# Attention, a Fourier mix and a feed-forward on one core: queries and keys loaded into both halves of the partitions, and weights that start later

## The chip, the core and the metric

The kernel runs on one core of a Trainium2 chip. Its engines work side by side, each through its own instruction stream in order: TensorE (PE, with its weight loads listed apart as PEld), VectorE (DVE), ScalarE (ACT), GpSimd (POOL) and SyncE (SP). SP, ACT and POOL also issue DMA transfers; 16 DMA engines carry them. The metric is the time of one execution on the device in microseconds (us); lower is better.

## The reference

For 8 batches of 8 heads, q, k and v are 576 x 64 in float32. Each head is attention with a mask by blocks of 64 rows; the heads side by side give x, 576 x 512 a batch. Then comes a two-dimensional Fourier transform of which the real part is added to x, a normalization and a feed-forward of 512 to 2048 to 512:

```python
scores = np.where(block_i >= block_j, q @ k.T / 8, -1e9)     # blocks of 64
attn = softmax(scores) @ v
x = attn.transpose(0, 2, 1, 3).reshape(B, S, H * D)
u = x + np.real(np.fft.fft(np.fft.fft(x, axis=1), axis=2))
un = (u - mean(u)) / np.sqrt(var(u) + 1e-6)
out = u + np.maximum(un @ w_ch1, 0) @ w_ch2
```

## The kernel before

**Precision.** TensorE gets rounded operands, so nearly every operand is held as a rounded part and the rest: probabilities, values, normalized rows and both weights as pairs of float16 (hi and lo), q and k as pairs of fp32r. A product is three matmuls (hi hi, hi lo, lo hi); for scores two suffice, since the pairs lie one above the other in the 128 partitions.

**A head.** `load_head` (L311) loads q and k of a head, transposed, 64 partitions x 1152 (288 KB). `lead` (L316) rounds both on ACT into LEAD, partitions 0 to 63; partitions 64 to 67 hold the mask. `lead_copies` (L319) copies the rounded q and k by two DMAs on SP into REST, each to the half in which the other's remainder will stand. `rest` (L324) writes the remainders there: q's on DVE, k's on POOL. LEAD and REST have two buffers, by the head's parity. `scores` (L391) multiplies REST with REST and LEAD with LEAD into PSUM, takes maxima on DVE (L411 to L416), exponentials on ACT twice (L425: float16 and float32) and their difference on POOL (L426). `turn` (L428) transposes the pair of float16 by a DMA on SP. `values` (L435) multiplies by the values' pair and scales by the sums of the rows (L463 to L466). After the second head of a pair the two columns go to x in DRAM (L471, L474).

**A batch.** When a batch's last pair is stored, `mirror` (L517) loads x again, plainly and with rows mirrored by indirect DMAs on POOL. `folded`, `stage1`, `stage2_sin` and `stage2_cos` (L538 to L632) do the transform over half the frequencies; the last step adds sums and differences to x: four additions a group, three groups a batch (L623 to L626), on DVE for batch 0 and on POOL for the others. `normalized_steps` (L670) normalizes and transposes on PE; each pair of row tiles then becomes a feed of 16 steps (`feed_steps`, L717), whose matmuls (h and acc) fill PE.

**The weights.** They are loaded as 64-bit words in 18 pieces (`weight_loads`, L813, from ACT), at most three ahead, into parts of W that are not yet needed and, for the last four, into `stage`. `weight_single` (L822) makes float32 of a piece in three DVE operations (L828 to L830) and sums its squares on ACT (L831). `weight_scale` (L836) gets a scale from the sums (once a weight), and `weight_parts` (L851) splits each of 2 x 16 chunks into hi and lo: the first weight by ACT, ACT and POOL (L855 to L859), the second by ACT and DVE (L855, L861). The first feed needs these chunks; heads of the second batch are not written before the last piece is (`"w32"`, L922).

**The order.** All this is written by a planner (L261 to L304, L910 to L958): lanes of steps with assumed costs for each engine and latencies ("D0.6" is 0.6 us of DVE, "L2.5" a latency of 2.5 us), keys that a step makes, keys that it comes after, and a place by which lanes are ranked. A step is issued when its assumed time has come; weights are squeezed in where DVE's or ACT's assumed queue is short. The framework then orders each engine's instructions once more by a simulation of its own, with the written order as rank and the data as the only hard condition. Matmuls alone keep the written order (`mm`, L201).

Of the kernel before, what the change touches and what calls it, by code (L numbers as in the profile page):

```python
# [37 lines left out]

FLIGHT = 3

PSHIFT = 5
# [144 lines left out]
def tile_attn_fourier_ffn(  # L186
# [14 lines left out]
    def mm(*args, **kw):  # L201
        return tc.keep_in_program_order(nc.tensor.matmul(*args, **kw))  # L202
# [28 lines left out]
    NB = 2  # L231
    LEAD = [const.tile([KM, 64 + 2 * S], F32R, name=f"lead{i}") for i in range(NB)]
    REST = [const.tile([P, 64 + 2 * S], F32R, name=f"rest{i}") for i in range(NB)]
    PROB = [[const.tile([P, 2, w], F16, name=f"prob{i}_{x}") for i, w in enumerate(WIDTHS)] for x in range(2)]
# [5 lines left out]
    for i in range(NB):  # L240
        nc.gpsimd.dma_start(LEAD[i][D:KM], c_masks)
        nc.vector.tensor_scalar(LEAD[i][0:D, 0:64], ones[0:D, 0:64], 0.0, None, op0=ALU.mult)
        nc.vector.tensor_scalar(REST[i][:, 0:64], ones[:, 0:64], 0.0, None, op0=ALU.mult)
    for n, blocks in enumerate(BLOCKS):
# [66 lines left out]
    def load_head(h):  # L311

        raws[h] = work.tile([D, 2 * S], F32, name="raw", bufs=2)
        nc.sync.dma_start(raws[h], qk[h])

    def lead(h):  # L316
        nc.scalar.copy(LEAD[h % NB][0:D, 64:], raws[h])  # L317

    def lead_copies(h):  # L319
        x0, x1 = REST[h % NB].bitcast(F32), LEAD[h % NB].bitcast(F32)  # L320
        nc.sync.dma_start(x0[D:P, 64:64 + S], x1[0:D, 64:64 + S])
        nc.sync.dma_start(x0[0:D, 64 + S:], x1[0:D, 64 + S:])

    def rest(h, which):  # L324

        x0, x1, raw = REST[h % NB], LEAD[h % NB].bitcast(F32), raws[h]
        if which == 0:
            nc.vector.tensor_tensor(x0[0:D, 64:64 + S], raw[:, 0:S], x1[0:D, 64:64 + S], op=ALU.subtract)  # L328
        else:
            nc.gpsimd.tensor_tensor(x0[D:P, 64 + S:], raw[:, S:], x1[0:D, 64 + S:], op=ALU.subtract)  # L330

# [59 lines left out]
    def scores(h, n):  # L391

        x0, x1 = REST[h % NB], LEAD[h % NB]
        prob = PROB[h % 2][n]
# [3 lines left out]
        for parts in SCORES[n]:  # L398
            t = ps_tile()
            at = 0  # L400
            for i, (j, lo, hi) in enumerate(parts):
                q, k = slice(P * j, P * (j + 1)), slice(64 + S + lo, 64 + S + hi)
                to = t[:, at:at + hi - lo]
                mm(to, x0[:, q], x0[:, k], start=(i == 0), stop=False, skip_group_check=True)
                mm(to, x1[:, q], x1[:, k], start=False, stop=(i == len(parts) - 1), skip_group_check=True)
                places.append((j, lo, hi, to))
                at += hi - lo
# [27 lines left out]
    def values(h, at):  # L435
# [32 lines left out]
        )  # L468
        if hh == 1:
            ds = slice(D * (n - 1), D * (n + 1))  # L470
            nc.sync.dma_start(  # L471
                xd[64:576, ds].rearrange("(c p) d -> p c d", p=P), x[:, 1:5].rearrange("p c h d -> p c (h d)")
            )
            nc.sync.dma_start(xd[0:64, ds], x[64:128, 0].rearrange("p h d -> p (h d)"))  # L474

# [19 lines left out]
    def value_lane():  # L495
        for h in range(B * H):
            for n in range(3):
                yield Step(
                    lambda n=n: values(h, n), (0.75, 0.38, 0.29)[n], ("D0.95",) if n == 2 else (),
                    (("S", h, n), ("N", h // 2)) + ((("V", h - 1, 2),) if h else ()), ("V", h, n),  # L500
                    need=(("d", h // H - 3, "u"),) if n == 2 and h >= 3 * H else (), place=h + 0.5,
                )
# [11 lines left out]
    def fourier_steps(b):  # L514
# [93 lines left out]
        def stage2_cos(c):  # L608
# [27 lines left out]
        yield Step(  # L636
            mirror, 0.0, ("G3", "L2.5"), (("V", H * b + H - 1, 2),), D_("u"),
            need=(("F", feed_number(b - 2, 1)),) if b > 1 else (), place=place,
# [14 lines left out]
        for c in (2, 0, 1):  # L653
            yield Step(lambda: stage2_sin(c), 0.67, ("A0.38",), (D_("zs"),), D_("b", c), True, place=place)
            yield Step(
                lambda: stage2_cos(c), 0.78, ("D0.86", "B", "D1.66" if b == 0 else "G3.0"), (D_("zc"), D_("zt"), D_("b", c)), D_("u", c), True,
                need=(("F", feed_number(b - 1, 2)),) if c == 2 and b == 4 else (), place=place,
            )
# [154 lines left out]
    def weight_loads(done):  # L813
# [6 lines left out]
        loads[0] = x  # L820

    def weight_single(x):  # L822
        if loads[0] <= x:
# [85 lines left out]

    lanes = [head_lane(), prepare_lane(), v_lane(), score_lane(), turn_lane(), value_lane(), transform_lane()]  # L910
    heads = [next(x) for x in lanes]
# [93 lines left out]
```

## Time and profile before

| what | value |
|---|---|
| median of 3 runs (lowest to highest) | 1315.21 us (1314.83 to 1320.55) |
| profiled execution: time, span | 1318.01 us, 1316.2 us |
| mean granted TensorE clock | 0.966 |
| busy: PE, DVE, ACT, POOL | 1125.2, 713.2, 620.6, 549.0 us |
| moved by DMA | 161.77 MB, of it 135.94 by SP's queue |

How to read it: busy times are sums over the span, and engines overlap. A row of the timeline gives start and length in us, engine, line, operation, output<-input, shape and count; brackets give the engine's idle time before it and what ended that. A name with q (SPq, ACTq) is an engine's sequencer, here mostly issuing DMAs. The DMA share is the mean busy share of the 16 DMA engines. L202 is the helper through which all matmuls are recorded, so they are told apart by tiles: ps, h and acc (PSUM banks, which scores also borrow), av for attention times values, wst for the weights' scale.

### The profile page before, as it was taken

The numbers are of one execution on the slowest core, as the hardware profiler recorded it, in microseconds if no ns is written. First come the engines' busy times: TensorE is split into PE (matmuls) and PEld (weight loads), VectorE is DVE, ScalarE is ACT, GpSimd is POOL, SyncE is SP. The second block draws the span as 40 slices with busy tenths as digits, with TensorE's granted clock in tenths as the row PEclk, the third lists the DMA queues.
The fourth block names the chain that finished last, engine by engine and source line by source line (L and its number), as shares of the span: only waits on it lengthen the run. The fifth ranks groups of instructions, "written<-read, shape, count | busy, mean of one in ns | idle before, by whom it ended". The sixth has DMA issues, their size and how long they took to land.

```text
span 1316.2 us, 25240 instructions
## 1 busy us (share of the span) xinstructions
PE 1125.2 (85%) x9620; PEld 826.4 (63%) x9620; DVE 713.2 (54%) x1697; ACT 620.6 (47%) x1329; POOL 549.0 (42%) x715
## 2 busy tenths in 40 slices
PE   1344175798989898989999999999999999999998
PEld 1244154575767676667767677667667767767665
DVE  7954477646465755576656656674673432412211
ACT  3645747764456543655666545665562211111110
POOL 2635725554455553536655366645741500300000
PEclk9999986798999998999999999999999999999999
DMA  9999607987568745765898567985863000000000
GB/s 320 230 203 237 176 5 141 163 172 151 96 148 152 172 85 130 144 152 116 173 193 165 108 120 191 173 167 114 172 119 82 26 16 17 21 1 17 16 17 16
DMA packets 307178, 161.77 MB, mean 123 GB/s; under 512 B 259281, under 2 KB 277857, under 8 KB 306929
## 3 DMA queue, kind: packets, MB, share of 16 engines
q1 hardware_dynamic: 300416, 135.94, 51.1%
q10 hardware_dynamic: 4384, 16.78, 3.9%
q0 software_dynamic: 2256, 7.45, 1.8%
q8 instruction: 75, 1.23, 0.4%
q14 instruction: 47, 0.38, 0.1%
HBM read 58.37 MB, written 18.87 MB: 59 GB/s over the span
## 4 chain that ended last, share of the span: by engine, by line
PE 52%; DVE 9%; DMA 8%; POOL 3%; issue 3%; ACT 2%; SPq 0%; DVEq 0%; POOLq 0%; ACTq 0%
PE h L202 20%; PE acc L202 20%; PE ps L202 8%; DMA turn<-prob 6%; PE av L202 3%; DVE M L411 2%; DMA u<-xd,rows 1%; DVE rest L328 1%; DVE tmp L541 1%; POOL prob L426 1%; PE ps L205 1%; ACT prob L425 1%; POOL rest L330 1%; ACT p L425 1%; DVE tmp L542 1%
## 5 line engine op out<-in xcount | busy, mean ns | idle before, releaser
L202 PE MATMUL h<-uh,W 128*128 128x256 f16 x2304 | 424.7, 276 | 0.0
L426 POOL TENSOR_TENSOR prob<-p,prob 128x288 f16<-128x288 f32 (+4 forms) x384 | 286.9, 754 | 276.2 <-ACT p L425 259.4
L202 PEld LDWEIGHTS <-W 128*128 128x128 f16 x3456 | 332.9, 99 | 67.1 <-issue 4.7
L202 PE MATMUL acc<-W,gh 128*128 128x512 f16 x1152 | 348.4, 384 | 0.0
L202 PE MATMUL h<-ul,W 128*128 128x256 f16 x1152 | 317.5, 276 | 0.0
L425 ACT ACTIVATE prob<-ps,M 128x64 f16<-128x64 f32 (+2 forms) x358 | 164.6, 493 | 138.6 <-DVE M L416 137.3
L742 DVE SCALAR_TENSOR_TENSOR gl<-h,gh 128x512 f16<-128x512 f32 x144 | 99.0, 687 | 238.6 <-ACT gh L741 238.2
L202 PE MATMUL acc<-W,gl 128*128 128x512 f16 x576 | 220.7, 383 | 1.1 <-DVE gl L742 0.6
L202 PE MATMUL av<-VH,turn 128*128 128x65 f16 x1920 | 130.7, 205 | 96.9 <-DMA turn<-prob 82.2
L741 ACT ACTIVATE gh<-h 128x512 f16<-128x512 f32 x144 | 86.7, 602 | 269.0 <-PE h L202 268.4
L202 PEld LDWEIGHTS <-turn 128*128 128x128 f16 x2880 | 116.9, 105 | 126.0 <-DMA turn<-prob 98.7
L411 DVE TENSOR_REDUCE M<-ps 128x1 f32<-128x288 f32 (+2 forms) x358 | 138.8, 426 | 88.1 <-PE ps L202 72.5
L425 ACT ACTIVATE p<-ps,M 128x64 f32<-128x64 f32 (+2 forms) x358 | 171.1, 494 | 15.1 <-POOL prob L426 12.5
L202 PEld LDWEIGHTS <-gh 128*128 128x128 f16 x1152 | 105.7, 100 | 97.1 <-issue 9.9
L330 POOL TENSOR_TENSOR rest<-raw,lead 64x576 fp32r<-64x576 f32 x64 | 106.9, 1671 | 115.7 <-ACT lead L317 89.4
L202 PE MATMUL ps<-rest 128*128 128x288 f32 (+2 forms) x358 | 123.7, 363 | 34.2 <-ACT p L425 26.6
L202 PE MATMUL av<-VL,turn 128*128 128x64 f16 x960 | 118.6, 204 | 0.0
L202 PEld LDWEIGHTS ps<-rest 128*128 128x128 f32 x358 | 73.8, 206 | 47.2 <-ACT p L425 32.3
L202 PE MATMUL ps<-lead 68*128 68x288 f32 (+2 forms) x358 | 103.3, 322 | 0.0
L202 PEld LDWEIGHTS <-gl 128*128 128x128 f16 x576 | 56.9, 99 | 71.5 <-issue 2.7
L317 ACT CAST lead<-raw 64x1152 fp32r<-64x1152 f32 x64 | 73.5, 1149 | 18.6 <-PE ps L202 18.4
L202 PEld LDWEIGHTS ps<-lead 68*128 68x128 f32 x358 | 74.3, 208 | 1.3
(166 smaller groups left out, 1197.2 us busy)
## 6 DMA issues: line engine op xcount, KB each, us to landing
raw<-in_qk_dram SPq DMA_DIRECT2D x64, 288.0 KB
rest<-lead SPq DMA_DIRECT2D x128, 144.0 KB
W<-in_moe_w_ch_dram ACTq DMA_DIRECT2D x14, 1024.0 KB
V<-in_v_dram SPq DMA_DIRECT2D x32, 320.0 KB
xd<-x SPq DMA_DIRECT2D x32, 256.0 KB
out_dram<-u SPq DMA_DIRECT2D x32, 256.0 KB
u<-xd SPq DMA_DIRECT2D x8, 512.0 KB
turn<-prob SPq DMA_TRANSPOSE x192
```

What stands on the lines that cost most here:

```text
L202: return tc.keep_in_program_order(nc.tensor.matmul(*args, **kw))
L205: return tc.keep_in_program_order(nc.tensor.transpose(*args, **kw))
L317: nc.scalar.copy(LEAD[h % NB][0:D, 64:], raws[h])
L328: nc.vector.tensor_tensor(x0[0:D, 64:64 + S], raw[:, 0:S], x1[0:D, 64:64 + S], op=ALU.subtract)
L330: nc.gpsimd.tensor_tensor(x0[D:P, 64 + S:], raw[:, S:], x1[0:D, 64 + S:], op=ALU.subtract)
L411: nc.vector.tensor_reduce(m[:, i:i + 1], x, axis=AX.X, op=ALU.max)
L425: nc.scalar.activation(to, x, AF.Exp, bias=bias[:, c:c + 1], scale=0.125)
L426: nc.gpsimd.tensor_tensor(pl, p32, ph, op=ALU.subtract)
L541: nc.vector.tensor_tensor(e[0:r], X[c][0:r], U[c][0:r], op=op)
L542: nc.vector.tensor_tensor(e[0:r, 1:256], e[0:r, 1:256], e[0:r, 511:256:-1], op=op)
L741: nc.scalar.activation(gh, t, AF.Relu)
L742: nc.vector.scalar_tensor_tensor(gl, t, 0.0, gh, op0=ALU.max, op1=ALU.subtract)
```

## The change

- The host hands q and k over twice, one below the other, and `load_head` loads 128 partitions (576 KB) instead of 64.
- `lead` rounds all 128 partitions into ONE (the old REST). The two DMA copies go. `lead_q` writes the rounded q into TWO (the old LEAD) by a copy on DVE from the raw q; `rest` writes q's remainder over the second half of ONE (DVE) and k's into TWO (POOL). Scores multiply ONE with ONE and TWO with TWO.
- Storing a pair of heads becomes a step of its own (`store_x`), in a lane of its own; a batch's `mirror` comes after the last of them, and the next pair's last `values` step after the one before.
- `weight_begin` writes one element of each of the first three landing places on DVE, from the raw tile of head 1 or the first V, so that these loads wait for those two. In the planner, piece x (0 to 7) is ranked after the last scores of head x (`AFTER`).
- The additions of batch 0 move from DVE to POOL.

```diff
+AFTER = (0, 1, 2, 3, 4, 5, 6, 7)
...
-        raws[h] = work.tile([D, 2 * S], F32, name="raw", bufs=2)
+        raws[h] = work.tile([P, 2 * S], F32, name="raw", bufs=2)
         nc.sync.dma_start(raws[h], qk[h])
     def lead(h):
-        nc.scalar.copy(LEAD[h % NB][0:D, 64:], raws[h])
-
-    def lead_copies(h):
-        x0, x1 = REST[h % NB].bitcast(F32), LEAD[h % NB].bitcast(F32)
-        nc.sync.dma_start(x0[D:P, 64:64 + S], x1[0:D, 64:64 + S])
-        nc.sync.dma_start(x0[0:D, 64 + S:], x1[0:D, 64 + S:])
+        nc.scalar.copy(ONE[h % NB][:, 64:], raws[h])
+
+    def lead_q(h):
+        nc.vector.tensor_copy(TWO[h % NB][0:D, 64:64 + S], raws[h][0:D, 0:S])
     def rest(h, which):
-        x0, x1, raw = REST[h % NB], LEAD[h % NB].bitcast(F32), raws[h]
+        x, raw = ONE[h % NB].bitcast(F32), raws[h]
         if which == 0:
-            nc.vector.tensor_tensor(x0[0:D, 64:64 + S], raw[:, 0:S], x1[0:D, 64:64 + S], op=ALU.subtract)
+            nc.vector.tensor_tensor(ONE[h % NB][D:P, 64:64 + S], raw[D:P, 0:S], x[D:P, 64:64 + S], op=ALU.subtract)
         else:
-            nc.gpsimd.tensor_tensor(x0[D:P, 64 + S:], raw[:, S:], x1[0:D, 64 + S:], op=ALU.subtract)
+            nc.gpsimd.tensor_tensor(TWO[h % NB][0:D, 64 + S:], raw[0:D, S:], x[0:D, 64 + S:], op=ALU.subtract)
...
-            yield Step(lambda: lead_copies(h), 0.0, ("Q1.2", "L2.2"), (("T", h),), ("TC", h), place=h - 0.9)
+            yield Step(lambda: lead_q(h), 0.0, ("D0.6",), (("L", h),), ("TC", h), place=h - 0.9)
...
+    def store_x(g):
+        b, n = divmod(2 * g, H)
+        xd, x, ds = xs[b], xs["pair"], slice(D * n, D * (n + 2))
+        nc.sync.dma_start(
+            xd[64:576, ds].rearrange("(c p) d -> p c d", p=P), x[:, 1:5].rearrange("p c h d -> p c (h d)")
+        )
+        nc.sync.dma_start(xd[0:64, ds], x[64:128, 0].rearrange("p h d -> p (h d)"))
+
+    def store_lane():
+        for g in range(B * H // 2):
+            yield Step(lambda: store_x(g), 0.0, ("Q1.1", "L2.0"), (("V", 2 * g + 1, 2),), ("XS", g), place=2 * g + 1.6)
...
-            engine = nc.vector if b == 0 else nc.gpsimd
+            engine = nc.gpsimd
...
+    def weight_begin():
+
+        for x in range(FLIGHT):
+            nc.vector.tensor_copy(raw(x)[0:1, 0:1].bitcast(F32), (raws[1][0:1, 0:1], vraw[0][0:1, 0, 0, 0:1])[x % 2])
+        weight_loads(0)
+
...
-        yield Step(lambda: weight_loads(0), 0.0, ("A1.2", "L5"), (("L", 0),), ("load",))
+        yield Step(weight_begin, 0.0, ("D0.4", "A1.2", "L6"), (("L", 1), ("LV", 0)), ("load",))
...
-                (("load",),), "w32" if x == len(LANDS) - 1 else None,
+                (("load",),) + ((("E", AFTER[x], 2),) if x < len(AFTER) else ()), "w32" if x == len(LANDS) - 1 else None,
...
+    qk = np.concatenate([qk, qk], 1)
```

More of the change, by code (lines that the diff above doesn't have):

```diff
@@ L231, in tile_attn_fourier_ffn @@
     NB = 2
-    LEAD = [const.tile([KM, 64 + 2 * S], F32R, name=f"lead{i}") for i in range(NB)]
-    REST = [const.tile([P, 64 + 2 * S], F32R, name=f"rest{i}") for i in range(NB)]
+    TWO = [const.tile([KM, 64 + 2 * S], F32R, name=f"two{i}") for i in range(NB)]
+    ONE = [const.tile([P, 64 + 2 * S], F32R, name=f"one{i}") for i in range(NB)]
     PROB = [[const.tile([P, 2, w], F16, name=f"prob{i}_{x}") for i, w in enumerate(WIDTHS)] for x in range(2)]
@@ L240, in tile_attn_fourier_ffn @@
     for i in range(NB):
-        nc.gpsimd.dma_start(LEAD[i][D:KM], c_masks)
-        nc.vector.tensor_scalar(LEAD[i][0:D, 0:64], ones[0:D, 0:64], 0.0, None, op0=ALU.mult)
-        nc.vector.tensor_scalar(REST[i][:, 0:64], ones[:, 0:64], 0.0, None, op0=ALU.mult)
+        nc.gpsimd.dma_start(TWO[i][D:KM], c_masks)
+        nc.vector.tensor_scalar(TWO[i][0:D, 0:64], ones[0:D, 0:64], 0.0, None, op0=ALU.mult)
+        nc.vector.tensor_scalar(ONE[i][:, 0:64], ones[:, 0:64], 0.0, None, op0=ALU.mult)
     for n, blocks in enumerate(BLOCKS):
@@ L391, in scores @@
     def scores(h, n):
-        x0, x1 = REST[h % NB], LEAD[h % NB]
+        x1, x2 = ONE[h % NB], TWO[h % NB]
         prob = PROB[h % 2][n]
@@ L403, in scores @@
                 to = t[:, at:at + hi - lo]
-                mm(to, x0[:, q], x0[:, k], start=(i == 0), stop=False, skip_group_check=True)
-                mm(to, x1[:, q], x1[:, k], start=False, stop=(i == len(parts) - 1), skip_group_check=True)
+                mm(to, x1[:, q], x1[:, k], start=(i == 0), stop=False, skip_group_check=True)
+                mm(to, x2[:, q], x2[:, k], start=False, stop=(i == len(parts) - 1), skip_group_check=True)
                 places.append((j, lo, hi, to))
@@ L500, in value_lane @@
                     (("S", h, n), ("N", h // 2)) + ((("V", h - 1, 2),) if h else ()), ("V", h, n),
-                    need=(("d", h // H - 3, "u"),) if n == 2 and h >= 3 * H else (), place=h + 0.5,
+                    need=((("d", h // H - 3, "u"),) if n == 2 and h >= 3 * H else ()) + ((("XS", h // 2 - 1),) if n == 2 and h > 1 else ()),
+                    place=h + 0.5,
                 )
```

12 lines of the change are left out of this document (3 added, 9 removed).

## The prediction, made before the changed kernel had run

> **What bounds the kernel now.** I read the page's forty slices first, then a table by stage, then the order of time inside the first stage.
>
> ```profile
> span 1316.2 us, 25240 instructions
> ...
> PE   1344175798989898989999999999999999999998
> ...
> DMA  9999607987568745765898567985863000000000
> ```
>
> ```profile
> 0.00:147.80 147.80, 53.55 (x468) 46.40 (x468) 91.99 (x197) 84.52 (x170) 73.65 (x100) 1.00 0.95 235
> 147.80:194.40 46.60, 22.17 (x105) 16.97 (x106) 33.11 (x71) 20.24 (x44) 17.09 (x24) 0.89 0.24 80
> 194.40:238.80 44.40, 26.48 (x230) 22.68 (x228) 33.92 (x83) 34.58 (x72) 24.03 (x28) 0.61 0.65 125
> 300.00:1000.00 700.00, 655.23 (x6123) 485.35 (x6122) 435.55 (x1098) 395.31 (x871) 369.02 (x477) 0.98 0.71 144
> 1000.00:1316.00 316.00, 311.51 (x2157) 214.19 (x2153) 85.27 (x155) 48.12 (x92) 30.86 (x52) 1.00 0.06 18
> ```
>
> The columns are the stretch, its length, the busy time of PE, PEld, DVE, ACT and POOL, the granted clock, the DMA share and GB/s. From 300 us on PE is busy 966.7 of 1016 us. Before 238.8 us it is busy 102.2, so 136.6 us are idle. The end therefore moves with the moment at which PE gets its full diet, less what PE did by then. This is the path to that moment:
>
> ```profile
> 147.79 0.38 SPq L471 DMA_DIRECT2D xd<-x  x1
> 148.77 0.85 ACTq L818 DMA_DIRECT2D u<-in_moe_w_ch_dram  x2
> 194.44 0.38 PE L202 MATMUL ps<-rest 128*128 128x288 f32 x1
> 210.93 0.56 PE L202 MATMUL ps<-wst,ones 128*128 128x1 f32 x2
> 237.68 1.07 DVE L861 SCALAR_TENSOR_TENSOR W<-W,wst 128x512 f16<-128x512 f32 x1
> ```
>
> The first batch's eight heads end at 147.8 us (the store of its last pair). Its transforms follow, and head 8's scores, which stand behind them in PE's written order, start at 194.4. The scale of the second weight is summed at 210.9, behind head 8's values, and the last part of that weight is ready at 238.8; from there both halves of the feed-forward run. Inside the first batch:
>
> ```profile
> 0.73 2.52 ACTq L818 DMA_DIRECT2D W<-in_moe_w_ch_dram  x4
> 1.64 0.60 SPq L314 DMA_DIRECT2D raw<-in_qk_dram  x1
> 6.23 0.69 DVE L828 TENSOR_SCALAR W<-W 128x1024 int32<-128x1024 int32 x1 [3.81 <-DMA W<-in_moe_w_ch_dram]
> 10.53 1.13 ACT L317 CAST lead<-raw 64x1152 fp32r<-64x1152 f32 x1
> 16.19 0.74 DVE L328 TENSOR_TENSOR rest<-raw,lead 64x576 fp32r<-64x576 f32 x1
> 19.66 0.58 PE L202 MATMUL ps<-rest 128*128 128x288 f32 x1 [0.78 <-DMA rest<-lead]
> 22.62 0.47 PE L202 MATMUL h<-lead 68*128 68x320 f32 x1
> 29.01 0.71 DVE L411 TENSOR_REDUCE M<-ps 128x1 f32<-128x288 f32 x2
> 40.72 7.74 SPq L430 DMA_TRANSPOSE turn<-prob  x3
> ```
>
> Head 0 needs 40.7 us to its first transpose, with weights in front of it on three queues; all eight heads then take 107 us more, 13.4 each, while the DMA engines are 95% busy.
>
> **The change part by part.**
>
> *Copies gone, start freed.* The rounded halves no longer go through SP's two copies (L321, L322), and weight loads 0 to 2 wait for the second head's load and the first V. The lead at 10.53 could start once raw has landed. The nearest row is the weight tile issued at 0.73 and used at 6.23, 5.5 us for 1 MB; so raw, issued at 1.64, is there by 7.1: at least 3.4 us. From the lead's end (11.7) to the scores (19.7) pass 8.0 us; without copies, and without conversions ahead of DVE's 0.74 us subtraction, about 2 remain: 6 us. From the scores' end (23.1) to the first maximum (29.0) DVE is busy with conversions and head 1: 5.9 us. Together 15.3 us. Later heads show the copies on the path too:
>
> ```profile
> 41.23 1.14 ACT L317 CAST lead<-raw 64x1152 fp32r<-64x1152 f32 x1
> 54.32 6.26 SPq L430 DMA_TRANSPOSE turn<-prob  x3
> 60.63 0.59 SPq L322 DMA_DIRECT2D rest<-lead  x1
> 71.15 0.58 PE L202 MATMUL ps<-rest 128*128 128x288 f32 x1 [3.63 <-ACT left L831]
> ```
>
> Head 3's lead ends at 42.4, but its second copy is issued 18 us later, behind three transposes on SP, and its scores start at 71.2. The engine named there, ACT, is a guess of the view; the copy is the later event.
>
> Against the whole gain stands the DMA share: 0.95 of 147.8 us, 140 us of work. A stretch with two copies and a raw load of 64 partitions (214.4 to 219.4, some transposes with them) and one with weight tiles of 128 partitions (2 to 6) moved:
>
> ```profile
> DMA packets 1680, 0.97 MB, mean 195 GB/s; under 512 B 1486, under 2 KB 1486, under 8 KB 1678
> DMA packets 595, 1.36 MB, mean 341 GB/s; under 512 B 191, under 2 KB 275, under 8 KB 595
> ```
>
> A head's 590 KB take 3.0 us now and, in one load over 128 partitions, 1.7 (estimates from these rates): 1.3 us a head, 13 us for the ten heads loaded by then. If the DMA engines bound every microsecond, the batch would gain these 13 less the up to 5.5 in which no weights flow at the start: 7.5. If waits bound, it gains the 15.3 and, behind it, the 13 as well: 28. I take the middle, **18**, since both stand in the rows: full DMA engines and a late head 0.
>
> *Sums of batch 0 on POOL.* Twelve additions move:
>
> ```profile
> L625 DVE TENSOR_TENSOR u<-u,dif x2: 406/406/406, 179.4 to 182.0; 128x257 f32<-128x257 f32 x2
> L625 POOL TENSOR_TENSOR u<-u,dif x14: 725/728/1122, 357.5 to 1129.0; 128x257 f32<-128x257 f32 x14
> ```
>
> 12 x (0.73 - 0.41) = 3.8 us, on the path between batch and restart. DVE loses 4.9 us of work there, so it could cost nothing; fully exposed POOL work would cost 8.8. I take **+4**: the normalization waits for the last sum.
>
> *The new copy of q on DVE, SP's queue freed.* A conversion step reads 1024 elements in 0.71 us (below), 0.4 for 576; the subtraction of that shape takes 0.74 at least:
>
> ```profile
> L330 POOL TENSOR_TENSOR rest<-raw,lead x64: 1390/1663/2521, 11.8 to 974.2; 64x576 fp32r<-64x576 f32 x64
> L328 DVE TENSOR_TENSOR rest<-raw,lead x64: 737/752/1972, 16.2 to 974.7; 64x576 fp32r<-64x576 f32 x64
> ```
>
> So 0.4 to 0.75 us a head, hidden behind ACT's lead of 1.13 in the batch. For 56 later heads it is 22 to 42 us on an engine that is busy 435.6 of 700, where PE lacks only 44.8 us. Against it SP loses two issues a head, and transposes stop standing behind copies:
>
> ```profile
> PEld L202 <- DMA turn<-prob: 38.0, 32, 5.1
> ```
>
> That is PE's wait for transposes from 300 to 1000. A tenth of it, 4 us, I count as won, 2 as lost to DVE: **-2**, with -15 and +10 as bounds.
>
> *The waits of the weights.* These are the costs of a conversion, and where one was moved:
>
> ```profile
> L830 DVE SCALAR_TENSOR_TENSOR W<-W 128x1024 int32<-128x1024 int32 x14 | 20.0, 1431 | 0.1
> L829 DVE SCALAR_TENSOR_TENSOR W<-W 128x1024 int32<-128x1024 int32 x14 | 19.7, 1405 | 0.2
> L828 DVE TENSOR_SCALAR W<-W 128x1024 int32<-128x1024 int32 x14 | 10.0, 713 | 18.6 <-DMA W<-in_moe_w_ch_dram 18.6
> ```
>
> ```profile
> 47.72 0.15 DVE L839 TENSOR_REDUCE wst<-ul 128x1 f32<-128x16 f32 x1
> 90.58 1.22 DVE L830 SCALAR_TENSOR_TENSOR W<-W 128x1024 int32<-128x1024 int32 x1
> 129.04 0.42 PE L202 MATMUL acc<-wst,ones 128*128 128x1 f32 x2
> ```
>
> The step for the first scale is written as one; its DVE part ran 81 us before its matmul. So the framework pulls work ahead wherever an engine has room, and the new place behind each head's scores ranks the conversions lower but does not hold them. Only the three loads really wait, by some 5 us, and the three one-element DVE writes that make them wait cost about 0.15 each. Cover: the fourteenth conversion ends at 92 us (the row at 90.58), 56 before the batch ends. Cost **0**; without the cover it is the third rival. The stores' own lane changes places in SP's order only: 0.
>
> Sum: -18 + 4 - 2 = -16. The profiled execution took 1318.0 us (span 1316.2 and 1.8 around it): 1302. The median of the runs shown, 1315.2, lies 2.8 below it, so **1299**.
>
> **The rivals.** *Hidden.* The restart hangs on the weights instead: the last four tiles are loaded only at 148.8 behind ACT's parts of the first weight, and the second scale waits for head 8. Then a batch that ends sooner waits, and some 5 of the 18 remain: 1312. For it speaks the row at 148.77; against it that DVE is free a third of that stretch.
>
> *More.* Waits bound the batch (28) and a third of PE's 44.8 us goes too (15): 1315 - 28 + 4 - 15 = 1276. For it speaks head 3, against it the DMA share.
>
> *Slower: conversions pile up behind the batch.* Place: DVE between batch and restart, 46.6 us with 33.1 busy, 13.5 free. Each conversion that slides there costs 0.71 + 1.41 + 1.43 = 3.55 us. From 8.3 on, (3.55 n - 13.5) exceeds the 16 won; eleven give 25.6 - 16 = +9.6, so 1325, all fourteen 1335. Lower rank and later loads speak for it; that six conversions written behind the batch's scores ran before 92 us speaks against it.
>
> *POOL held up.* While DVE's and POOL's subtractions overlap they stretch (0.74 to 1.97, 1.39 to 2.52). Should the copy of q do the same to POOL's work, 0.4 to 0.75 us for 56 heads is 22 to 42 us on the way to the transposes; a third of it at PE gives 7 to 14, so 1310.
> The Trainium skill, page "SBUF — State Buffer", section "Who interferes with whom", says that a copy in a two-port mode takes the port pair that VectorE shares with GpSimd for the whole instruction and the other engine blocks. The stretched rows agree that one waits for the other.
>
> **How the numbers follow.** Forecast 0.45 (own range 1286 to 1309: batch 10 to 28), hidden 0.18, more 0.10, piled up 0.19, POOL 0.08. A measurement here tells about 0.5%, 6.6 us, from no change: below 1308.6 is faster, above 1321.8 slower. Faster: 0.42 of the forecast, "more", 0.02 of POOL: 0.54. Same: 0.03 + 0.15 + 0.04 and 0.02 of the pile: 0.24. Slower: the remaining 0.22 (0.17 pile, 0.03 hidden, 0.02 POOL). The range, 1276 to 1328, leaves out the worst of the pile and gains beyond both bounds.
>
> **What would show it.** Right: the first transpose near 25 us instead of 40.7, the last pair's store near 130, head 8's scores near 180, the last L861 near 224, with 300 to 1000 as dense as now. Wrong: a store at 147 again (DMA bound), a store at 130 but scores at 194 (hidden), conversions L828 to L830 after the store (pile), longer L426 or L330 rows (POOL), or a PE share after 300 us that moves by more than 1%.

## The result, and the profile after

The changed kernel is slower: 1384.6 us median of four runs (1369.4 to 1393.2) beside 1316.1 for the kernel before on the same chip. The ratio is 1.043, 95% interval 1.036 to 1.049, so some 56 us; it goes by the two faster of the four runs (1369.4 and 1376.7), while the median counts all four. The profiled execution took 1376.7 us. The forecast was 1299, with a range up to 1328.

The forty slices of the changed kernel:

```profile
span 1374.8 us, 24975 instructions
...
PE   2343257998769999897979799898989999999998
...
DMA  9998424786676468545777756675361010000000
```

PE rises to 9 one slice sooner than before, and then falls back, to 7 and 6 in the eleventh and twelfth slice (344 to 412 us) and to 8 and 7 again and again until 1000 us. The DMA row still starts with nines. By stages (the columns are those of the prediction's table):

```profile
0.00:143.70 143.70, 50.62 (x468) 44.88 (x468) 103.84 (x210) 73.39 (x151) 68.26 (x91) 0.76 0.96 246
143.70:186.00 42.30, 15.73 (x73) 12.21 (x73) 25.98 (x40) 27.62 (x56) 27.00 (x25) 0.56 0.26 85
186.00:225.60 39.60, 19.18 (x170) 17.39 (x170) 32.76 (x73) 27.41 (x52) 25.01 (x34) 0.66 0.40 92
300.00:1000.00 700.00, 615.60 (x5580) 457.44 (x5580) 456.21 (x1094) 381.05 (x835) 359.93 (x465) 0.93 0.64 139
1000.00:1374.00 374.00, 367.20 (x2619) 254.15 (x2619) 111.12 (x215) 67.49 (x134) 44.28 (x71) 1.00 0.11 26
```

From 300 to 1000 us PE is busy 615.6 us, where it was 655.2: 40 us less, at a lower granted clock too (0.93 against 0.98), with 5580 PE records against 6123. DVE is busy 456 instead of 436. What was left undone comes at the end: the last stretch holds 367 us of PE, 56 more than before. The loss lies behind 300 us: until then PE is busy 157.1 us, where it was 158.5. Over the whole span PE is busy 1139.9 us instead of 1125.2, for the same 9620 records, and idle 235 instead of 191; so of the 59 us of span some 44 are idle time of PE, and 15 are matmuls that took longer by the profile. Whether the lower clock is a cause of its own was not tested; executions of the kernel before took 1307.4 us at a mean clock of 0.941 and 1322.8 at 0.963. (The granted clock is lower in the first three stretches as well, 0.76 in the first, where it was 1.00; PE idles 93 of its 143.7 us anyway.)

The path that the prediction followed, in the changed kernel's order of time:

```profile
12.42 0.61 PE L203 MATMUL ps<-one 128*128 128x288 f32 x1 [0.99 <-DVE one L329]
13.68 1.39 DVE L412 TENSOR_REDUCE M<-ps 128x1 f32<-128x288 f32 x4 [0.27 <-PE ps L203]
21.83 5.01 SPq L431 DMA_TRANSPOSE turn<-prob  x1
143.30 0.38 SPq L474 DMA_DIRECT2D xd<-x  x1
185.96 0.40 PE L203 MATMUL acc<-one 128*128 128x288 f32 x1
187.46 0.28 PE L203 MATMUL ps<-wst,ones 128*128 128x1 f32 x2
224.16 1.40 DVE L875 SCALAR_TENSOR_TENSOR W<-W,wst 128x512 f16<-128x512 f32 x2
```

The start is as forecast: the first scores at 12.4 instead of 19.7, the first maximum at 13.7 instead of 29.0, the first transpose at 21.8 instead of 40.7. But the last pair's store comes at 143.3, only 4.5 us sooner. Head 8's scores come at 186.0 (194.4), and the last part of the second weight is done at 225.6, 13 us sooner than 238.8. The restart is early, as the prediction wanted, and it is worth nothing.

PE's waits for transposes from 300 to 1000 us (us in all, times, longest) have nearly doubled; they were 38.0 for the weight loads and 28.7 for the matmuls:

```profile
PEld L203 <- DMA turn<-prob: 71.4, 37, 5.5
PE av L203 <- DMA turn<-prob: 54.8, 32, 5.2
```

And the feeds (the two halves of the feed-forward) stop for a while. Busy time and count of ACT's relu (L741 before, L749 after), which runs once for two blocks of the feed-forward, in the kernel before and in the changed one:

```profile
280.00:340.00 60.00, 4.22 (x7) 0.91 0.81 158
340.00:400.00 60.00, 3.59 (x6) 1.00 0.53 115
```

```profile
280.00:340.00 60.00, 4.20 (x7) 0.94 0.74 161
340.00:400.00 60.00, 0.63 (x1) 0.71 0.70 153
```

Batch 0's two feeds end at 276 and 355 us instead of 310 and 388, and the third at 474 instead of 451. From 340 to 400 us PE has heads and transforms only.

### The profile page after: what moved, and what is told of

The parts are those of the page before. It is cut to its first block, busy times and chain, and to the rows that moved or that the text cites. A ratio compares the mean times of both kernels' runs of the same rounds, so it can differ in the third digit from the quotient of the medians.

```text
span 1374.8 us, 24975 instructions
## 1 busy us (share of the span) xinstructions
PE 1139.9 (83%) x9620; PEld 838.5 (61%) x9620; DVE 775.6 (56%) x1752; ACT 623.9 (45%) x1329; POOL 561.0 (41%) x727
## 4 chain that ended last, share of the span: by engine, by line
PE 50%; DVE 16%; DMA 14%; POOL 7%; issue 7%; ACT 5%; SPq 1%; DVEq 0%; POOLq 0%; ACTq 0%
PE acc L203 19%; PE h L203 19%; DMA turn<-prob 8%; PE ps L203 7%; PE av L203 3%; POOL prob L427 3%; DVE M L412 3%; DVE one L329 2%; DMA W<-in_moe_w_ch_dram 2%; ACT prob L426 2%; ACT p L426 1%; POOL two L331 1%; DMA raw<-in_qk_dram 1%; DVE tmp L549 1%; DVE W L844 1%
## 5 line engine op out<-in xcount | busy, mean ns | idle before, releaser
L427 POOL TENSOR_TENSOR prob<-p,prob 128x288 f16<-128x288 f32 (+4 forms) x384 | 292.6, 769 | 313.8 <-ACT p L426 308.1
L426 ACT ACTIVATE prob<-ps,M 128x64 f16<-128x64 f32 (+3 forms) x346 | 159.6, 493 | 158.1 <-DVE M L417 157.5
L749 ACT ACTIVATE gh<-h 128x512 f16<-128x512 f32 x144 | 86.5, 601 | 269.8 <-PE h L203 269.7
L426 ACT ACTIVATE p<-ps,M 128x64 f32<-128x64 f32 (+3 forms) x346 | 165.8, 493 | 18.6 <-POOL prob L427 16.3
L412 DVE TENSOR_REDUCE M<-ps 128x1 f32<-128x288 f32 (+3 forms) x346 | 133.4, 426 | 63.0 <-PE ps L203 47.6
L331 POOL TENSOR_TENSOR two<-raw,one 64x576 fp32r<-64x576 f32 x64 | 99.4, 1553 | 103.7 <-ACT one L320 85.7
L203 PE MATMUL ps<-one 128*128 128x288 f32 (+3 forms) x346 | 122.2, 368 | 16.0 <-ACT p L426 13.1
L203 PE MATMUL ps<-two 68*128 68x288 f32 (+3 forms) x346 | 102.2, 329 | 0.0
L203 PEld LDWEIGHTS ps<-one 128*128 128x128 f32 x346 | 73.9, 214 | 28.4 <-ACT p L426 19.5
L320 ACT CAST one<-raw 128x1152 fp32r<-128x1152 f32 x64 | 73.8, 1154 | 30.2 <-PE ps L203 17.5
L329 DVE TENSOR_TENSOR one<-raw,one 64x576 fp32r<-64x576 f32 x64 | 83.9, 1311 | 3.7 <-ACT one L320 1.5
```

Of the source, the lines that this page charges most:

```text
L320: nc.scalar.copy(ONE[h % NB][:, 64:], raws[h])
L329: nc.vector.tensor_tensor(ONE[h % NB][D:P, 64:64 + S], raw[D:P, 0:S], x[D:P, 64:64 + S], op=ALU.subtract)
L331: nc.gpsimd.tensor_tensor(TWO[h % NB][0:D, 64 + S:], raw[0:D, S:], x[0:D, 64 + S:], op=ALU.subtract)
L412: nc.vector.tensor_reduce(m[:, i:i + 1], x, axis=AX.X, op=ALU.max)
L426: nc.scalar.activation(to, x, AF.Exp, bias=bias[:, c:c + 1], scale=0.125)
L427: nc.gpsimd.tensor_tensor(pl, p32, ph, op=ALU.subtract)
```

## The experiments

Two things differ after 300 us: the **work** (one more DVE operation in each head, another form of load) and the **order** in which the planner writes the steps down. The planner works from estimated durations and waits, so each edit of these makes it write another order, for PE as well, whose order is kept as written. To tell the two apart, the planner's loop was replaced by a list of its own decisions in some kernels (the banks of PSUM included). The list fixes PE's order: the 9620 matmuls stand in one and the same order in the kernels that share a list. The framework still places the other engines' instructions by its own simulation, and there they move. In the double load below, for instance, some 210 of the 1697 other DVE operations stand elsewhere than in the kernel before. So "the work" includes what the framework made of it.

```
-    while True:
-        ... the planner picks the next step
+    for x in ORDER.split():
+        ... the next step of the lane that the list names
+        issue(step)
```

In kernels that take the order of the kernel before, the conversions stand where they stood there and not behind the scores of heads 0 to 7. Line numbers differ from kernel to kernel, since the list stands in the file. Times below are ratios to the kernel before on the same chip, with the 95% interval; 1% is 13 us.

**The double load alone, in the order of before.**

```
     before's order, from the list
+    qk loaded twice; lead rounds 128 partitions; lead_q on DVE
-    lead_copies on SP
```

> Edit: queries and keys loaded twice and the copy of q on DVE (with the copies on SP gone), nothing else; the steps are written down in exactly the order that the kernel before has, from a list, instead of by the planner. Theory 'order' (the loss after 300 us comes from the order in which PE's work is written, which the planner made anew from the changed costs): 1295 to 1318 us, PE busy in 300 to 1000 us about 655 again. Rival 'work' (the loss comes from the new DVE copy, DVE +62 us busy, and from raw loads that hold SP's queue while they wait for DVE, 59 us after 300): 1350 to 1380 us, with about 615 of PE in that stretch. Rival 'sums and waits' (POOL's sums or the waits of the weights are the cause): 1295 to 1318, as the order theory; the next kernel tells these two apart.

Measured: 1361.8 us, 1.034 (1.026 to 1.042). The work alone costs some 45 us with PE's order unchanged. PE is busy 633.6 us from 300 to 1000 us, 22 less than before, and 149.4 instead of 158.5 ahead of that.

**The order alone, with all the work of before.**

```
     the kernel before
+    the changed kernel's order, from a list
```

> Edit: the kernel before with all its work (copies on SP, sums of batch 0 on DVE, weights loaded at once, stores within the values), but its steps written down in exactly the order that the changed kernel's planner found, from a list. Theory 'order': 1355 to 1390 us, as slow as the changed kernel, with the PE hole between 300 and 430 us (103.8 of 130 busy there). Rival 'work': 1305 to 1325. Rival 'sums and waits': 1305 to 1325 as well, since neither the sums nor the waits are in it.

Measured: 1362.8 us, 1.034 (1.028 to 1.040). From 300 to 1000 us:

```profile
300.00:1000.00 700.00, 616.67 (x5587) 458.48 (x5585) 417.60 (x1056) 380.53 (x838) 366.76 (x469) 0.93 0.68 141
```

That is the changed kernel's loss (615.6), with DVE busy no longer than before (417.6, where it was 435.6). PE waits for transposes as long as in the changed kernel:

```profile
PEld L265 <- DMA turn<-prob: 72.0, 40, 5.8
PE av L265 <- DMA turn<-prob: 61.7, 33, 5.7
```

So these waits, which stood out in the profile after, come with the order alone, while SP's raw loads wait for DVE's subtraction only 5.0 us there. The order costs as much by itself as the work. Neither theory alone was right, and the two do not add up: both together are 1.043.

**All parts in the order of before, and the double load in an order of its own.**

> Edit: the changed kernel with all its parts (loads twice, copy of q on DVE, the first weight loads waiting for the second head and the first V, sums on POOL, stores as own steps), written down in the order of the kernel before; so the conversions no longer stand behind the scores of heads 0 to 7. Theory 'order': 1295 to 1320. Rival 'work': 1350 to 1385. Rival 'sums and waits': 1340 to 1380 if POOL's sums or the waiting loads cost the time, 1295 to 1318 if it is the conversions' place.

Measured: 1358.7 us, 1.030 (1.023 to 1.037), beside 1.043 (1.036 to 1.049) in the changed kernel's own order. The intervals touch. With all the work in place, the changed kernel's own order adds some 13 us, and not the 44 that it costs on the old work.

> Edit: queries and keys loaded twice and the copy of q on DVE, nothing else, with the order left to the planner. In the order that it finds, the second feed of batch 0 and the third feed are again far apart. Theory 'order': slower than before, 1340 to 1400. Rival 'work': 1350 to 1380. Rival 'sums and waits': 1295 to 1318. It tells the third from the other two.

Measured: 1382.2 us, 1.049 (1.043 to 1.055): as slow as the changed kernel, without POOL's sums or any wait of the weights. "Sums and waits" are not needed for the loss.

**What in the double load costs the time?** In the kernels with the double load SP's raw loads wait for DVE's subtraction far more than before, where the same wait came to 6.5 us from 300 to 1000 us (of the changed kernel):

```profile
SPq L315 <- DVE one L329: 59.4, 26, 13.0
```

So "SP's queue" was a rival to "DVE". First a useless copy on DVE was added to the kernel before:

```
+        nc.vector.tensor_copy(lead rows 96 to 127, raws[h][0:32, 0:S])
```

> Edit: the kernel before, in its own order and with its copies on SP, plus one useless copy on DVE for each head (32x576 of raw into rows of lead that nothing reads; a copy's time goes by the 576 elements of a row, not by the rows). It measures the new DVE copy by itself. Theory 'DVE's turn' (the copy stands ahead of the subtraction on DVE, the subtraction then starts after POOL's and has to wait until POOL pauses): slower by 15 to 45 us, 1330 to 1360, with the subtraction's mean from 300 to 1050 us well over its 1.09 us. Rival 'SP's queue' (the loss of the copied order came from raw loads that wait for DVE's subtraction and hold the transposes, while nothing stood in their way before): 1312 to 1325, since SP still has its copies between lead and the next raw load.

Measured: 1371.9 us, 1.041 (1.039 to 1.043), more than expected and not by the mechanism expected. DVE's groups of that kernel (busy us, mean ns, then the idle time ahead and its cause):

```profile
L394 DVE TENSOR_TENSOR one<-raw,two 64x576 fp32r<-64x576 f32 x64 | 64.6, 1009 | 4.3 <-ACT two L382 4.2
L385 DVE CAST two<-raw 32x576 fp32r<-32x576 f32 x64 | 38.0, 594 | 113.4 <-DMA raw<-in_qk_dram 112.7
```

The subtraction is as fast as ever (1009 ns); but DVE stands 112.7 us in front of the copy, waiting for a raw load that had not landed. It needs only raw, so it was put early in DVE's queue. Hence this run is a case of its own, and a second one made the copy wait for ACT's lead, as the subtraction does:

```
+        nc.vector.tensor_copy(lead rows 96 to 127, lead[0:32, 64:64 + S])
```

> Edit: the kernel before in its own order, plus one useless copy on DVE for each head that reads lead (32x576), so that it waits for ACT's lead as the subtraction does, and not for the load of raw, which the first such copy had waited for (90 us of DVE's time from 300 to 1050 us). It measures the copy's time on DVE by itself. Theory 'the copy's own time costs': 1330 to 1350, half to all of 0.5 us x 64 heads. Rival 'only a wait in front of it costs': 1313 to 1325.

Measured: 1350.2 us, 1.024 (1.018 to 1.030). DVE waits for the lead 9.3 us in all; the copy takes 837 ns, and the subtraction behind it 1301 instead of 1059:

```profile
L394 DVE TENSOR_TENSOR one<-raw,two 64x576 fp32r<-64x576 f32 x64 | 83.3, 1301 | 1.7
L385 DVE CAST two<-two 32x576 fp32r<-32x576 f32 x64 | 53.6, 837 | 11.0 <-ACT two L382 9.3
```

DVE gets 69 us more to do (53.6 and 83.3 - 67.8) and the kernel takes 32 longer, with SP's two copies still in place and SP's raw loads waiting for the subtraction only 20 us (300 to 1000 us). One short operation for each head is far from hidden, though DVE was busy only 62% of the stretch.

**The copy taken off DVE.**

```
-        nc.vector.tensor_copy(TWO[h % NB][0:D, 64:64 + S], raws[h][0:D, 0:S])
+        nc.sync.dma_start(TWO[...][0:D, 64:64 + S], ONE[...][0:D, 64:64 + S])
```

> Edit: queries and keys loaded twice, in the order of the kernel before, but q's rounded half is brought to the second tile by one copy on SP from the first tile, instead of by DVE. Theory 'DVE's turn': back to 1295 to 1322. Rival 'SP's queue': the raw load still stands behind DVE's subtraction in SP's queue, 1340 to 1365.

Measured: 1336.0 us, 1.013 (1.010 to 1.016), between the two expectations. Of the 45 us, 28 (16 to 39) are gone with DVE's copy, and SP's wait for the subtraction fell with it (26 us from 300 to 1050 us, where it was 71). 17 us remain, and the subtraction is still slow. Its group in the double load with DVE's copy (first fence) and without it:

```profile
L391 DVE TENSOR_TENSOR one<-raw,one 64x576 fp32r<-64x576 f32 x64 | 96.6, 1510 | 3.1 <-ACT one L382 1.0
L385 DVE CAST two<-raw 64x576 fp32r<-64x576 f32 x64 | 35.2, 551 | 3.4 <-PE ps L264 3.3
```

```profile
L391 DVE TENSOR_TENSOR one<-raw,one 64x576 fp32r<-64x576 f32 x64 | 94.0, 1469 | 12.3 <-ACT one L382 10.6
```

**Why is the subtraction slow?** One of the longest, in the order of time, DVE and POOL of the double load in the order of before:

```profile
438.32 0.45 DVE L385 CAST two<-raw 64x576 fp32r<-64x576 f32 x1
...
439.06 4.30 DVE L391 TENSOR_TENSOR one<-raw,one 64x576 fp32r<-64x576 f32 x1
```

```profile
439.12 0.51 POOL L597 MEMSET u<- 1x512 f32 x1
439.61 1.39 POOL L393 TENSOR_TENSOR two<-raw,one 64x576 fp32r<-64x576 f32 x1
440.97 1.77 POOL L489 TENSOR_TENSOR prob<-p,prob 128x448 f16<-128x448 f32 x2
```

DVE's 0.75 us of work ends at 443.36, 0.62 us behind the end of POOL's run (442.74). The same distance stands in every kernel: over the subtractions longer than 1 us in which a run of POOL ends, the median from that end to the end of DVE's subtraction is 0.61 to 0.62 us. In the kernel before, POOL's run was short:

```profile
479.53 1.41 POOL L330 TENSOR_TENSOR rest<-raw,lead 64x576 fp32r<-64x576 f32 x1 [0.31 <-POOL U L625]
481.01 1.12 POOL L625 TENSOR_TENSOR u<-u,dif 128x257 f32<-128x257 f32 x1
```

```profile
479.83 1.71 DVE L328 TENSOR_TENSOR rest<-raw,lead 64x576 fp32r<-64x576 f32 x1
```

Between POOL's two operations lie 0.07 us (480.94 to 481.01). DVE begins there, ends at 481.54, and this time POOL's second operation is the one that is stretched (1.12 instead of 0.73). In the double load POOL's next operation begins before the last has ended (440.97, when the one ahead ends at 441.00), and DVE gets in only when POOL runs dry. It is not always so:

```profile
731.09 1.61 DVE L391 TENSOR_TENSOR one<-raw,one 64x576 fp32r<-64x576 f32 x1
```

```profile
730.69 1.39 POOL L393 TENSOR_TENSOR two<-raw,one 64x576 fp32r<-64x576 f32 x1 [0.87 <-ACT one L382]
732.06 1.30 POOL L489 TENSOR_TENSOR prob<-p,prob 128x320 f16<-128x320 f32 x1
```

Here DVE got its turn after POOL's first operation (its end, 732.70, lies 0.62 us behind 732.08), and POOL's next one took 1.30 us instead of the 0.78 usual in such a run. In this kernel POOL ended an operation, with the next right behind it, 29 times while a subtraction longer than 1 us stood there: 23 times DVE had to wait on, 6 times it got in. Over the subtractions longer than 1 us of all traces it got in at 65 of 206 such ends, and at 532 of 536 ends that left a gap. What decides without a gap was not found. The cause of the gap is a wait: before, the instruction behind POOL's subtraction waits for POOL's own work in 56 of 64 cases; with the double load in none.

The Trainium skill, page "SBUF — State Buffer", section "Who interferes with whom", says that an operation of VectorE with two inputs in SBUF contends with GpSimd's reads for a shared port pair, an exclusive lock, and that the order of issue decides who blocks. The rows agree that one waits while the other works. With the order of issue they do not go: DVE's subtraction began at 439.06, and POOL's operations of 439.61 and 440.97 were still served ahead of it.

So a wait was put back, on the very instruction behind POOL's subtraction, where it could be (44 and 46 of 64 cases), with PE's order as it was. The framework moved some of the other engines' operations, of DVE's 8 in the first kernel and 79 in the second, so the first is the cleaner test:

```
+    tc.add_manual_dep(<the operation that follows on POOL>, <POOL's subtraction>, Sync)
```

> Edit: as the kernel with the double load, q's half by one copy on SP and the order of before; in addition the instruction that follows POOL's subtraction on POOL waits for that subtraction to have ended (as it does in the kernel before), so POOL's run of back-to-back work has a short gap there. Theory 'DVE is locked out by POOL' (DVE's subtraction begins only when POOL's unbroken run has ended: it ended 0.61 us behind the run in the traces so far): the subtraction is never over 2.0 us, its mean falls from 1.47 to 1.1, and the time from 1336 to 1313 to 1325. Rival 'SP's queue or the load': the time stays at 1330 to 1342, whatever the subtraction does.

> Edit: as the kernel with the double load and the copy of q on DVE in the order of before, with the same short gap behind POOL's subtraction. Theory 'DVE is locked out by POOL': the subtraction's mean falls from 1.51 to about 1.1 us and the time from 1362 to about 1340 to 1350; what is left over the kernel before is the copy itself. Rival 'SP's queue or the load': 1355 to 1368.

Measured: without DVE's copy 1326.2 us, 1.007 (1.004 to 1.010), where it was 1.013 (1.010 to 1.016); with it 1340.3, 1.019 (1.015 to 1.024), where it was 1.034 (1.026 to 1.042). The groups:

```profile
L403 DVE TENSOR_TENSOR one<-raw,one 64x576 fp32r<-64x576 f32 x64 | 75.5, 1180 | 12.2 <-ACT one L394 10.3
```

```profile
L403 DVE TENSOR_TENSOR one<-raw,one 64x576 fp32r<-64x576 f32 x64 | 79.4, 1240 | 2.6 <-ACT one L394 0.3
L397 DVE CAST two<-raw 64x576 fp32r<-64x576 f32 x64 | 38.9, 607 | 2.6 <-PE ps L266 1.7 <-DMA raw<-in_qk_dram 0.9
```

Both means fell, by 0.29 and 0.27 us, and the time by some 8 and 20 us; the first comes out just above its expected range, the second at the lower end of it. Single subtractions still take up to 3.5 and 4.0 us (two and one are over 2.0 us, where 14 were in each), which the theory had excluded: some heads got no gap, and gaps elsewhere on POOL are missing too. In this order a POOL that pauses and lets DVE in is worth more than one that never waits. With DVE's copy out and most of the long subtractions gone, 9 us of the double load's 45 remain unexplained.

The same step on the kernel before, POOL's subtraction cut in two:

> Edit: the kernel before, with POOL's subtraction cut into two halves of 288 columns, the second of which waits for the first, so that DVE can begin in the middle. Theory 'DVE locked out by POOL': DVE's subtraction is never over 1.4 us, its mean falls from 1.06 to 0.9, and the time by 5 to 10 us: 1306 to 1312. Rival 'POOL pays the same in two starts': 1314 to 1322.

Measured: 0.999 (0.997 to 1.001), no change. The mean fell to 908 ns as expected and DVE's busy time from 300 to 1000 us by 8 us, but POOL's grew there (385 instead of 369), and PE's stayed (654 and 655). So a shorter subtraction does not by itself buy time. (This kernel, too, is written from the list: the list as such costs nothing.)

**The three other parts.** Without the double load, in the planner's own order and in that of before:

> Edit: the changed kernel without the double load: queries and keys as in the kernel before (64 partitions, two copies on SP, no copy on DVE), but with the waits of the weights, the sums on POOL and the stores as own steps; order left to the planner, which finds one like that of the kernel before (no hole). Theory 'order and DVE's turn, both': 1300 to 1325. Rival 'sums and waits': 1340 to 1380.

> Edit: the changed kernel without the double load (64 partitions, two copies on SP), with the first weight loads waiting, the sums on POOL and the stores as own steps, in the order of the kernel before. Theory 'order and DVE': these three parts cost nothing by themselves, 1308 to 1322, and the 32 us that they cost in the planner's own order are that order's. Rival 'sums and waits': 1335 to 1360.

Measured: 1350.0 us, 1.026 (1.023 to 1.028) in its own order; 1327.3, 1.009 (1.005 to 1.013) in the order of before. There PE is as dense as ever from 300 to 1000 us:

```profile
300.00:1000.00 700.00, 656.18 (x6076) 485.06 (x6075) 435.98 (x1104) 396.27 (x870) 372.74 (x478) 0.97 0.70 144
```

So waits, sums and stores together cost some 12 us, ahead of 300 us (PE busy 148.0 against 158.5 by then): the last pair's store comes 3 us later than before, the first normalization at 186 instead of 181, and the last part of the second weight is ready at 247 instead of 239. The other 22 go with the order.

All parts, with q by one copy on SP, in the planner's order; and with the gap, in the order of before:

> Edit: the changed kernel with all its parts, only q's rounded half comes by one copy on SP instead of by DVE; order left to the planner. In the order that it finds the third feed follows the second by about as much as in the kernel before (no hole). Theory 'order and DVE's turn, both': 1295 to 1325, both causes gone at once. Rival 'SP's queue' or 'sums and waits': 1340 to 1375.

> Edit: the changed kernel with all its parts, but q's half by one copy on SP, the gap behind POOL's subtraction, and the order of the kernel before. Theory 'DVE and order, nothing else': what is left is a few us for the sums on POOL, 1316 to 1332. Rival 'the first batch's gain comes through once DVE is free': under 1310.

Measured: 1370.5 us, 1.037 (1.031 to 1.044), and 1346.1, 1.023 (1.019 to 1.027). Both expectations failed. In the first the third feed ends 83 us behind the second (63 before, 119 in the changed kernel), a hole of 20 us at most, and it is slow all the same. The second lost its time ahead of the first feed's end (321 us, 305 with the double load and gap alone): the last conversion's last step begins at 119 us (91 before) and the last pair's store comes at 156. Why the parts cost more together than one by one was not found.

**What is wrong with the order?** The hole between 340 and 400 us was the first suspect; and the lock was tried in the changed kernel's own order.

```
+                    if f == 0 and part == 0:
+                        after += (("E", 12, 2),)
```

> Edit: the changed kernel; in the planner's list the first step of the first feed may come only behind the scores of head 12, so that batch 0's feeds are not used up before batch 1's transform. Theory 'the hole is what the order costs': 1355 to 1372, and gh no longer stops between 340 and 400 us. Rival 'the order costs in every head, the hole is paid back by the earlier feeds': 1376 to 1395, with the hole gone and the other feeds no nearer to each other.

> Edit: the changed kernel in its own order, with the short gap behind POOL's subtraction in 52 of the 64 heads and nothing else. Theory 'DVE locked out by POOL, and the order': the lock's part goes here too, 10 to 21 us less than the changed kernel: 1358 to 1376, and the hole without feeds (340 to 400 us) stays. Rival 'the lock only matters in the order of before': 1376 to 1392.

Measured: 1389.7 us, 1.056 (1.052 to 1.059), and 1379.5, 1.048 (1.044 to 1.051). The hole is gone in the first of them (the relu from 280 to 400 us):

```profile
280.00:340.00 60.00, 3.64 (x6) 0.94 0.69 152
340.00:400.00 60.00, 4.20 (x7) 1.00 0.61 125
```

and the kernel is no faster: the eight feeds behind the second take 74 us each, where they took 68 before (414 to 1009 against 388 to 928 us). The hole was paid for by the earlier feeds; the loss is spread. The gap is worth nothing that shows in this order (1.048 and 1.043 overlap), although the subtraction's mean fell from 1311 to 1172 ns.

Last, the kernel before with its planner's constants changed by a trifle:

```
-HOP = 0.25                                       -    ("D0.95",) if n == 2 else (),
+HOP = 0.26                                       +    ("D0.97",) if n == 2 else (),
```

> Edit: the kernel before with one constant of its planner changed by a trifle: the time that it assumes between two engines is 0.26 us instead of 0.25. All the work is the same; the order in which the steps are written is the same up to step 283 of 2990 (about where the feeds begin) and another one behind it. Theory 'any new draw of the order is worse than the one of before': 1330 to 1365. Rival 'the order of the changed kernel is bad for what the change put into it': 1308 to 1324.

> Edit: the kernel before with the planner's estimate of DVE's work behind the values raised from 0.95 to 0.97 us, and nothing else; the written order again departs at step 283 of 2990. Theory 'any new draw of the order is worse than the one of before': 1330 to 1365. Rival 'the order of the changed kernel is bad for what the change put into it': 1308 to 1324.

Measured: 1335.6 us, 1.013 (1.009 to 1.016), and 1349.1, 1.023 (1.021 to 1.026). Same work, an order that is the same for the first 283 of 2990 steps, and 17 and 30 us more. The stretch for the two:

```profile
300.00:1000.00 700.00, 647.52 (x5915) 476.60 (x5913) 432.00 (x1093) 391.39 (x865) 371.79 (x473) 0.95 0.71 142
```

```profile
300.00:1000.00 700.00, 635.22 (x5801) 470.78 (x5799) 424.08 (x1075) 383.16 (x844) 365.95 (x463) 0.94 0.68 140
```

PE loses 8 and 20 us here, DVE does not gain work. So the order of the kernel before is a good draw: the three other orders of the same work that were tried, these two and the changed kernel's, were slower by 1.3 to 3.4%. Which property makes an order good was not found; the one hole is excluded as the only reason.

No kernel beat the one before.

## Why the prediction was wrong

The steps in the prediction's own order:

- **What bounds the kernel.** The reading was that the end moves with the moment at which PE gets its full diet. The moment came sooner (last weight part 225.6 instead of 238.8, "near 224" had been named), and the end came 56 us later. That PE stays as dense from 300 us on was taken as given, and it is what broke.
- **"Copies gone, start freed": -18.** The first maximum came 15.3 us sooner, the very sum, but partly by luck: 7.2 us up to the first scores, where 9.4 had been worked out, and 8.1 behind them instead of 5.9. The batch gained 4.5 us, less than the lower bound of 7.5, so the term was too large. The DMA share is 0.96 of that stretch again, at 246 instead of 235 GB/s. That the DMA engines bound it fits the share; no run took their work away, so it is argued. The 13 us at the restart nearly match the 14 of the forecast (18 - 4) by luck, since 9 of them were gained behind the batch.
- **"Sums of batch 0 on POOL": +4,** "the waits of the weights" and the stores, 0. Together with each other they measured +12 (7 to 16) in the order of before. Sums of 4 fit; the rest would fall where the zeros stand, on the late first batch and weights, but no run took the three apart.
- **"The new copy of q on DVE, SP's queue freed": -2, bounds -15 and +10.** This is the step whose failure turned the sign. By itself, with PE's order unchanged, the double load cost 45 us, where 10 was the bound on that side. DVE's copy is some 28 of it; that POOL shuts DVE out longer, 8 to 20 (the two overlap). The copy's price was nearly right (551 ns against the 0.4 to 0.75 worked out). What was wrong is the assumption that an engine busy 436 of 700 us hides it: 69 us added to DVE cost the kernel 32. And SP was not freed: its queue lost the copies, but then its raw loads waited for DVE's late subtraction (59.4 us instead of 6.5).
- **The missing step.** The change was costed in the order of before. Several estimates and dependencies of the planner were edited, so PE's program was another one: from its 27th matmul on the order is not that of before. That order costs 44 us on the old work, and two trifles cost 17 and 30. No term of the sum stood for it, and the range had no place for it either; the stores' own lane was put at 0 because it "changes places in SP's order only". These two steps do not account for all of it: with DVE's copy out, the gap in and the order of before, the kernel with all its parts still took 1346.1 us, some 30 over the kernel before, and the cause of those stays open.
- **The rivals.** "Conversions pile up behind the batch" did not happen in the changed kernel: the last step of the fourteenth begins at 105 us, in a batch that ends at 143. "POOL held up" had the right pair of engines and the wrong one waiting: the mean of POOL's subtraction went from 1671 to 1553 ns, that of DVE's from 1059 to 1311. Its 1310 was too small, since it was worked out for POOL's 0.4 to 0.75 us. "Hidden" did not come either: it let the batch end 18 us sooner and the restart 5, and the batch gained 4.5 and the restart 13. The test named at the end, a PE share after 300 us that moves by more than 1%, is what came: 615.6 against 655.2 is 6%.

## What to carry to other kernels

When a program's order is made by a planner from estimates, cost an edit twice: the work, and a new draw of the order; run the old order with the new work, and the new order with the old work, before arguing from either. If the order of the kernel before happens to be a good draw, an edit that touches an estimate starts behind, here by 1.3 to 3.4%. An engine that is busy 62% of the time was no cover for a short operation that stands in each round's chain; look at what is queued behind it, and which engine then gets ahead of it.

## What the runs showed of the hardware

DVE's subtraction of two tensors in SBUF did not run beside POOL's operations and did not always get its turn after one of them: when POOL's next operation followed without a gap, it had to wait on at 141 of 206 ends, up to 4.30 us in all for 0.75 us of work. It ended 0.61 to 0.62 us behind the end of the POOL operation that it had waited for, in all kernels. A pause of 0.07 us on POOL was enough to let it in (532 of 536 ends with a gap); then POOL's next operation took 1.12 instead of 0.73 us. A wait on POOL for its own last operation makes such a pause. Putting it back saved 8 and 20 us in the order of before, and nothing that shows in the changed kernel's order or, by the cut in two, in the kernel before.
